# Sparse attention and a gated feed-forward on one core: a re-ordered lead-in, smaller weight pieces, a finer first output stage, and the last batch's transposes asked for earlier

## The chip, the cores and the metric

The kernel runs on one core of a Trainium2 chip. The metric is the time of one execution in microseconds on the device; of several runs the median is taken. One further execution was recorded by the hardware profiler. Times inside it count from the start of its span.

## The reference

Four batches of eight heads, 768 positions, head size 64. Every position attends to its neighbours within 15 positions and to one summary of each block of 32 positions: the summary key is the maximum over the block, the summary value the mean, and log 32 is added to its score. The joined heads go through a feed-forward with a gelu of the form h * sigmoid(1.702 h), without residual.

```python
k_sum = k.reshape(B, H, nb, block, D).max(axis=3)
v_sum = v.reshape(B, H, nb, block, D).mean(axis=3)
mask_l = np.abs(pos[:, None] - pos[None, :]) < window
scores_s = scale * np.einsum('bhsd,bhnd->bhsn', q, k_sum) + np.log(block)
a = softmax(concatenate([where(mask_l, scores_l, -1e9), scores_s]))
attn = np.matmul(a, concatenate([v, v_sum], axis=2))
x = attn.transpose(0, 2, 1, 3).reshape(B * S, H * D)     # 3072 x 512
h = x @ w_in                                             # 512 x 2048
out = (h / (1.0 + np.exp(-1.702 * h))) @ w_out           # 2048 x 512
```

q, k and v are 6.3 MB each in float32, the two weight matrices 4.2 MB each. Loads that are issued by GpSimd (POOL) change float32 to bfloat16 or float16 on the way.

## The kernel before, in words

The work is one long program, written out in the order in which each engine is to run it: every instruction of an engine stays in its program order. A batch is cut in two halves of 384 positions. "Pair" p is two heads (p = 0 to 3).

**Lead-in.** Batch 0, first half, is done pair by pair: keys and queries are turned on TensorE (`k_turn`, `q_turn`), copied from PSUM by ScalarE (ACT) or VectorE (DVE) (`k_own`, `q_copy`), the block maxima are taken on DVE (`k_max`), then scores (`s_bias`, `s_own`, `s_edges`), exponentials on ACT (`s_exp`), block scores (`b_turn`, `b_exp`), the sums of values over blocks as matmuls with a selector matrix E (`v_sum`, `v_copy`), products with values (`av_own`, `av_edges`, `av_blocks`), normalisation on DVE (`v_norm`), the turn of the result x (`x_turn`, `x_copy`), and the first two column groups of the first layer (`ff_first`). Matmuls on an array of zeros (`idle`) fill TensorE's waits at the start. The keys of pairs 0 and 1 come through SP's queue in float32 and are cast on ACT (`cast_k0`); all else comes through POOL's queue, in program order.

**First half of batch 0, feed-forward.** `ff_in(0, (nt,))` makes column group nt (128 of 2048) of the first layer: four matmuls of 384 columns and a gelu on ACT. The output stage `ff_out(0, ms, part)` takes row group ms (of three) and a quarter of the 2048 rows of w_out (four matmuls of 512 columns); it runs quarter by quarter, three row groups each, 12 slots. Beside these slots, `plan0` places the attention of batch 0's second half: late query turns ("q", `q_late`), scores ("s"), values and normalisation ("v"), the turn of x ("x", `tx`). Then `ff_in(1, ...)` runs the first layer of the second half, with the turns of batch 1's keys and queries between (`todo`), and `ff_out(1, ...)` its output, with batch 1's attention beside it (`plan1`).

**Batches 1 to 3.** Feed-forward of batch b with the attention of batch b + 1 beside the output products (`plan`); both layers' weights or sums of them enter a seven-product scheme (`w_sum`, `g_sums`, `product`). Keys, queries and x of batches 2 and 3 are turned by DMA transposes that SP issues: `xk` for keys, `xq` for queries, `dx` for x. SP issues strictly in order, and it issues the output stores and the DMAs that copy value rows (`value_rows`) too.

**Loads.** POOL issues, in this order: queries, keys and values of batch 0, w_in in five pieces, w_out in quarters with the four late query loads of batch 0 (`load_q1`) after the first quarter, the masks' arithmetic (`finish_masks`) ahead of the last quarter, then batch 1 (`load_batch(1)`). The program uses eight completion semaphores for these loads in turn, so that an issue waits for the landing of the load eight places ahead of it. Later batches are loaded by `load_batch(b)`, called from the output stage of the batch before; for batch 3 it waits (`gate2`) until batch 2's queries are turned.

Of the kernel before, what the change touches and what calls it, by code (L numbers as in the profile page):

```python
# [35 lines left out]
def kernel(  # L36
# [47 lines left out]
    RQ = 4  # L84
# [60 lines left out]
    E = consts.tile([128, EX + 128], BF16, name="E")  # L145
    ident16 = consts.tile([128, 128], F16, name="ident16")
    warm = lead.tile([128, 512], BF16, name="warm")
# [12 lines left out]
    def selectors():  # L160
        dve.memset(E, 0.0)
        for g in range(4):
            dve.memset(E[32 * g:32 * g + 32, EX + g:EX + g + 1], 1.0)

# [97 lines left out]
    def load_w_out(c):  # L262
        wo = moe_w_out.rearrange("(nt ni) d -> ni nt d", ni=128)
        pool.dma_start(out=w_out_sb[:, c * 4:(c + 1) * 4, :],
                       in_=wo[:, c * 4:(c + 1) * 4, :])
# [32 lines left out]
    def idle(n, cols=128):  # L298
# [82 lines left out]
    def k_turn(p):  # L381
        ps = st["K", p] = pturn.tile([128, 1024], BF16, name="ps_k", tag="turn")
        o = 2 * (p % 2)
        turn_plain(ps[:, 0:S], kb2[p // 2][:, o:o + 2])
# [16 lines left out]
    def q_turn(p):  # L401
        if p % 2 == 0:
            st["Q2"] = pturn.tile([128, 1024], BF16, name="ps_q", tag="turn")
        st["Q", p] = st["Q2"][:, p % 2 * HALF:p % 2 * HALF + HALF]
# [78 lines left out]
    def v_sum(ps_):  # L483

        for p in ps_:
            if p == 0:
                t = pturn.tile([128, 512], F32, name="ps_vt", tag="turn")
                st["VT", 0], st["VT", 1] = t[:, 0:2 * D], t[:, 2 * D:4 * D]
                st["VT", 0, 1] = t[:, 0:4 * D]
            elif p > 1:  # L490
                st["VT", p] = pturn.tile([128, 512], F32, name="ps_vt", tag="turn")[:, 0:2 * D]
            for i in range(2):
                for j in range(NJ):
                    o = EX - (p % 2 * 2 + i) * 32 - 4 * j
                    pe.matmul(out=st["VT", p][:, i * D:(i + 1) * D], lhsT=E[:, o:o + 128],
                              rhs=v0n[:, 2 * p + i, j, 0:D],
                              start=(j == 0), stop=(j == NJ - 1), skip_group_check=True)

    def v_copy(ps_, eng):
        h0, n = 2 * ps_[0], 2 * len(ps_)  # L500
        copy(eng, vs4[:, h0:h0 + n, 0:D], st[("VT",) + ps_].rearrange("p (h d) -> p h d", d=D))
# [367 lines left out]
    def ff_out(u, ms, part):  # L869
        if part == 0:  # L870
# [5 lines left out]
        if part == 3:  # L876
# [7 lines left out]
    gate3 = consts.tile([128, 2], F32, name="gate3")  # L884
    dve.memset(gate, 0.0)
# [9 lines left out]
    dve.memset(warm, 0.0)  # L895
# [25 lines left out]
    bands()  # L921
    dve.memset(v0n[:, :, :, D:VC], 1.0)
    clear_sums(dve)
    dve.tensor_copy(out=ident16, in_=ident)
# [10 lines left out]
    q_turn(1)  # L935
    s_bias(1)
    q_copy(0, dve)
    q_copy(1, dve)
    k_max(0)
    idle(8)  # L940
    s_own(0)
    s_own(1)
    s_edges(0)
    s_exp(0)
    s_edges(1)
    s_exp(1)
    k_max(1)
    k_turn(2)
    k_own(2, dve)
    b_turn(0)  # L950
    k_turn(3)
    k_own(3, act)
    b_exp(0)
    q_turn(2)
    q_turn(3)
    q_copy(2, dve)
    q_copy(3, dve)
    k_max(2)
    k_max(3)
    s_bias(2)  # L960
    s_bias(3)
    s_own(2)
    s_own(3)
    s_edges(2)
    s_exp(2)
    s_edges(3)
    s_exp(3)
    v_sum((0,))
    b_turn(1)
    b_exp(1)  # L970
    v_sum((1,))
    v_copy((0, 1), dve)
    av_own(0)
    av_own(1)
    av_edges(0)
    av_edges(1)
# [4 lines left out]
    v_sum((2,))  # L981
    v_copy((2,), act)
    av_own(2)
    av_edges(2)
    av_blocks(2)
    v_norm(2)
    v_sum((3,))
    v_copy((3,), act)
    av_own(3)
    av_edges(3)  # L990
    x_turn(0)
    x_copy(0, act)
    av_blocks(3)
    v_norm(3)
    x_turn(1)
    x_copy(1, act)
    x_turn(2)
    x_copy(2, act)
    ff_first(0)
    gelu_soon()  # L1000
    x_turn(3)
    ff_first(1)
    x_copy(3, dve)
    ff_first(2)
# [25 lines left out]
    plan0 = {1: ["q0", "q1", "q2"], 2: ["q3", "s0", "s1"], 4: ["s2", "s3"], 6: ["v0", "v1"], 8: ["x0"], 9: ["x1"]}  # L1030
# [221 lines left out]
```

## Time and profile before

| | |
|---|---|
| runs (us) | 206.19 (median), 205.59, 206.76 |
| profiled execution | 205.72 us, of which the span 203.7 |
| granted TensorE clock | 0.998 of full speed |
| lead-in, to the first whole first-layer group | about 0 to 20.7 us |
| batch 0: first half's first layer and output, second half's first layer and output | 20.7 to 29.8, to 44.5, to 57, to 74 |
| batch 1, batch 2, batch 3 (feed-forward) | from 74, 119, 163 |
| after the last matmul | about 3 us |

An engine's row in the profile gives its busy time, its share of the span and its number of instructions. PE is TensorE's matmuls, PEld its weight loads, SP the queue engine that does nothing but issue. A row of the chain of waits is start, duration, engine and what it writes, with the count of merged instructions. In the page's DMA row each digit is the busy share, in tenths, of the 16 DMA engines in one of 40 equal slices (5.1 us each). A row by windows gives the stretch, its length, busy time and count of PE, PEld, DVE, ACT and POOL, granted clock, DMA share and GB/s. Rows of a single load give the issuing engine, the load, the issue's duration (ns) and the first and last time of issue; the row under them gives the time from issue to landing (least, median, most). Rows "A <- B: total, times, longest" say that A stood idle until B was done.

### The profile page before, as it was taken

To read this page: it belongs to the slowest core of one execution; us is meant where nothing else is said; L and a number is where in the kernel's file an instruction comes from. 1 tells how busy PE (TensorE), PEld (TensorE's weight loads), DVE (VectorE), ACT (ScalarE), POOL (GpSimd) and SP (SyncE) were. 2 spreads that over 40 slices of the span, in tenths; PEclk is the share of its full clock that TensorE was granted. 3 is DMA by queue.
4 is the path that set the end of the run, shared out by engine and by line. 5 is a ranking of instruction groups with operands and counts; after the bars stand their busy time and mean duration, and the time that the engine had idled before them with its cause. 6 is when DMAs were issued, how large, how long until landed. Compare 5 with 4: busy or idle time off the path is not lost.

```text
span 203.7 us, 5850 instructions
## 1 busy us (share of the span) xinstructions
PE 196.8 (97%) x2358; PEld 136.7 (67%) x2358; DVE 141.6 (70%) x391; ACT 125.4 (62%) x240; POOL 90.3 (44%) x141
## 2 busy tenths in 40 slices
PE   6899999999999999999999999998999999999993
PEld 6567554556754665665888965666888855668882
DVE  6776885594855874897768689895769567758221
ACT  4674875539777617777871546778580568984220
POOL 7955489456899592002974035000000019870000
PEclk9999999999999999999999999999999999999999
DMA  6999999999999999999999979999022940000223
GB/s 179 159 164 204 207 210 218 184 156 240 107 157 149 185 181 165 139 162 156 118 185 146 154 125 137 130 241 180 0 106 52 172 140 3 0 0 0 106 105 103
DMA packets 95994, 28.13 MB, mean 138 GB/s; under 512 B 83664, under 2 KB 93152, under 8 KB 95968
## 3 DMA queue, kind: packets, MB, share of 16 engines
q0 software_dynamic: 69648, 13.24, 82.1%
q1 hardware_dynamic: 26176, 14.39, 34.9%
q8 instruction: 18, 0.29, 0.6%
q10 hardware_dynamic: 144, 0.13, 0.2%
q14 instruction: 8, 0.07, 0.1%
HBM read 27.26 MB, written 6.29 MB: 165 GB/s over the span
## 4 chain that ended last, share of the span: by engine, by line
PE 82%; DMA 9%; DVE 5%; ACT 1%; issue 1%; SPq 0%; ACTq 0%; DVEq 0%
PE ph L28 23%; PE poA L28 16%; PE po L28 11%; PE poB L28 8%; PE ps_av L28 4%; PE phA L28 4%; DMA out_dram<-osb 4%; PE poC L28 4%; PE ps_s L28 3%; DMA qT<-qb 3%; DMA gT<-in_k_dram 2%; DVE ks L28 2%; PE ps_t L28 1%; PE ps_x L28 1%; DVE qT L28 1%; DVE gs L28 1%
## 5 line engine op out<-in xcount | busy, mean ns | idle before, releaser
L28 PE MATMUL ph<-xT,w_in_sb 128*128 128x384 f16 x400 | 67.6, 326 | 0.1
L28 PEld LDWEIGHTS <-w_in_sb 128*128 128x128 f16 x442 | 42.7, 98 | 27.1 <-issue 0.2
L28 ACT ACTIVATE gT<-ph 128x384 f16<-128x384 f32 x100 | 47.9, 492 | 17.9 <-PE ph L28 17.1
L28 PEld LDWEIGHTS <-gT 128*128 128x128 f16 x312 | 28.8, 98 | 11.0
L28 ACT ACTIVATE a_sb<-ps_s 128x768 bf16<-128x768 f32 (+1 forms) x32 | 25.0, 826 | 12.1 <-PE ps_s L28 12.1
L28 PEld LDWEIGHTS <-gs 128*128 128x128 f16 x288 | 27.7, 98 | 3.4
L28 POOL DMA_DIRECT2D vw<-in_v_dram x36 | 24.6, 704 | 11.2 <-DMA kb<-in_k_dram 4.1
L28 POOL TENSOR_TENSOR gs<-gT 128x384 f16<-128x384 f16 x8 | 7.3, 911 | 43.1 <-PE phC L28 42.0
L28 PE MATMUL po<-w_out_sb,gT 128*128 128x512 f16 x96 | 23.6, 380 | 0.0
L28 DVE TENSOR_TENSOR a_sb<-a_sb,mk 128x768 bf16<-128x768 bf16 x28 | 14.9, 554 | 6.5 <-ACT a_sb L28 5.9
L28 PE MATMUL poA<-ws,gs 128*128 128x256 f16 x144 | 18.7, 273 | 0.0
L28 DVE TENSOR_TENSOR x<-ps_av,rc 128x384 f16<-128x384 f32 x32 | 17.8, 558 | 1.1
L28 DVE TENSOR_TENSOR gs<-gT 128x384 f16<-128x384 f16 (+1 forms) x34 | 13.3, 390 | 7.2 <-ACT gT L28 6.9
L28 POOL DMA_DIRECT2D qb<-in_q_dram x16 | 15.1, 964 | 3.1 <-DMA v0n<-in_v_dram 1.7
L28 PEld LDWEIGHTS <-kx 64*128 64x128 bf16 (+1 forms) x378 | 10.0, 95 | 7.8 <-issue 4.9
L28 DVE TENSOR_REDUCE ks<-kx 128x24 bf16<-128x768 bf16 x12 | 11.4, 948 | 3.4 <-ACT kx L28 3.2
L28 POOL DMA_DIRECT2D kb<-in_k_dram x14 | 13.6, 987 | 0.3 <-issue 0.3
L28 ACT ACT_TABLE_LOAD x10 | 12.8, 1283 | 1.0 <-PEq L1236 0.8
L28 ACT ACTIVATE osb<-poA 128x256 f32<-128x256 f32 x9 | 3.5, 384 | 15.8 <-PE poA L28 15.8
L28 ACT ACTIVATE s<-poA 128x256 f32<-128x256 f32 x11 | 4.2, 385 | 11.2 <-PE poA L28 11.2
L28 PEld LDWEIGHTS <-a_sb 128*64 128x64 bf16 (+2 forms) x400 | 7.8, 108 | 2.8 <-issue 1.3
L28 PE MATMUL poA<-w_out_sb,gT 128*128 128x256 f16 x72 | 9.4, 273 | 0.0
(117 smaller groups left out, 288.9 us busy)
## 6 DMA issues: line engine op xcount, KB each, us to landing
out_dram<-osb SPq DMA_DIRECT2D x22, 256.0 KB, 3.7
kb<-in_k_dram POOLq DMA_DIRECT2D x14, 192.0 KB, 6.6
qb<-in_q_dram POOLq DMA_DIRECT2D x12, 192.0 KB, 10.3
vw<-in_v_dram POOLq DMA_DIRECT2D x36, 64.0 KB, 5.5
w_out_sb<-in_moe_w_out_dram POOLq DMA_DIRECT2D x4, 512.0 KB, 13.0
w_in_sb<-in_moe_w_in_dram POOLq DMA_DIRECT2D x3, 512.0 KB, 12.8
vw<-vs SPq DMA_DIRECT2D x6, 198.0 KB, 6.7
gT<-in_k_dram SPq DMA_DIRECT2D x2, 384.0 KB, 3.5
```

The source lines that it names most:

```text
L28: r = f(*a, **kw)
```

## The change

- **Lead-in.** The keys of pairs 0 and 1 are cast into the layout in which two heads lie side by side, so that a turn takes 6 transposes of 128 x 128 (`turn_tiles`) instead of 12 of 128 x 64. The first half's queries lie as three rows on each of 128 partitions instead of four on 96. The array of zeros is float32, and the 40 idle matmuls (28, 4 and 8 of 128 columns) become 4 of 256 columns, 3 and 1 of 128. The block sums of values of pairs 0 and 1 are made by one run of six matmuls of 256 columns with a wider selector (`E4`), followed by a multiplication on DVE with a mask (`own`) that keeps each head's rows. `bands` on DVE moves behind the other constants; each pair's scores and exponentials follow each other; the first block scores (`b_turn(0)`) and the products with values take other places; x is turned earlier for pairs 0 and 1.
- **Weights.** w_in is loaded in eight pieces of 256 columns instead of two of 256 and three of 512; the first half of w_out in four pieces of two row groups, its second half in two quarters, with late queries between.
- **First output stage.** 24 slots of two matmuls instead of 12 of four. The second half's attention is spread over them anew. The last turn of x (x1) is taken out of it and put into `ff_in(1, range(3))`, between the first and the second half of the sums over the 512 input features.
- **Sums of w_out.** `w_sum` (DVE) moves to later places.
- **Batch 2's keys.** The first half of their load is issued beside `ff_in(1, (11,))` instead of in `load_batch(2)`.
- **Batch 3.** `xk` is called after products 8 and 10 instead of 16 and 18 of batch 1's output, `xq` after the third step of batch 2's first layer instead of the fifth.

POOL's loads around the weights, before:

```order
L28 DMA v0n<-in_v_dram 128x12x64 x4
L28 DMA w_in_sb<-in_moe_w_in_dram 128x4x256 x2
L28 DMA w_in_sb<-in_moe_w_in_dram 128x4x512 x3
L28 DMA w_out_sb<-in_moe_w_out_dram 128x4x512
L28 DMA qb<-in_q_dram 128x2x192 x4
L28 DMA w_out_sb<-in_moe_w_out_dram 128x4x512 x2
L28 MEMSET mk 128x128
```

Now (qb are the late queries; mk, the first row of the masks' arithmetic):

```order
L28 DMA v0n<-in_v_dram 128x12x64 x4
L28 DMA w_in_sb<-in_moe_w_in_dram 128x4x256 x8
L28 DMA w_out_sb<-in_moe_w_out_dram 128x2x512 x2
L28 DMA qb<-in_q_dram 128x2x192 x2
L28 DMA w_out_sb<-in_moe_w_out_dram 128x2x512
L28 MEMSET mk 128x128
```

and behind the masks' arithmetic, now:

```order
L28 AFFINE_SELECT mk<-mk 32x64
L28 DMA w_out_sb<-in_moe_w_out_dram 128x2x512
L28 DMA qb<-in_q_dram 128x2x192 x2
L28 DMA w_out_sb<-in_moe_w_out_dram 128x4x512 x2
L28 DMA kb<-in_k_dram 128x12x64 x4
L28 DMA qb<-in_q_dram 128x12x64 x2
```

where only the last quarter of w_out stood before. The pieces are smaller and half of the late queries stand later, but the second half of w_out still comes behind all of w_in, the first half of w_out and the four late query loads.

SP's queue in the output stage of batch 1, before (xT are the four x transposes for batch 2, kx the key transposes of batch 3, qT ahead of them the queries of batch 2):

```order
L28 DMA_TRANSPOSE qT_90<-qb 128x12x128 x2
L28 DMA out_dram<-osb 128x512 x2
L28 DMA_TRANSPOSE xT_98<-x_2258 128x6x128
L28 DMA out_dram<-osb 128x512
L28 DMA_TRANSPOSE xT_99<-x_2290 128x6x128
L28 DMA out_dram<-osb 128x512
L28 DMA_TRANSPOSE xT_100<-x_2355 128x6x128
L28 DMA_TRANSPOSE xT_101<-x_2387 128x6x128
L28 DMA_TRANSPOSE kx_89<-kb 128x12x64 x4
L28 DMA out_dram<-osb 128x512 x2
```

Now:

```order
L28 DMA_TRANSPOSE qT_92<-qb 128x12x128 x2
L28 DMA out_dram<-osb 128x512 x2
L28 DMA_TRANSPOSE kx_91<-kb 128x12x64 x4
L28 DMA_TRANSPOSE xT_100<-x_2211 128x6x128
L28 DMA out_dram<-osb 128x512
L28 DMA_TRANSPOSE xT_101<-x_2243 128x6x128
L28 DMA out_dram<-osb 128x512
L28 DMA_TRANSPOSE xT_102<-x_2308 128x6x128
L28 DMA_TRANSPOSE xT_103<-x_2340 128x6x128
L28 DMA out_dram<-osb 128x512 x2
```

The four key transposes moved from behind the last x transpose to ahead of the first.

The diff, cut to its core:

```diff
-    RQ = 4
+    RQ = 3
...
     def cast_k0(p):
         if p == 0:
-            kb2[0] = castp2.tile([128, 4, RK, D], BF16, name="kb", tag="kb")
-        act.activation(out=kb2[0][:, 2 * p:2 * p + 2].rearrange("p h r d -> p h (r d)"), in_=k0f[p], func=ACT.Copy)
+            kb2[0] = castp2.tile([128, 2, RK, 2, D], BF16, name="kb", tag="kb")
+        act.activation(out=kb2[0][:, p].rearrange("p r h d -> p h r d"),
+                       in_=k0f[p].rearrange("p h (r d) -> p h r d", d=D), func=ACT.Copy)
...
-    warm = lead.tile([128, 512], BF16, name="warm")
+    warm = lead.tile([128, 256], F32, name="warm")
...
+            dve.memset(E4[32 * g:32 * g + 32, 20 + g:20 + g + 97:32], 1.0)
+            dve.memset(own[32 * g:32 * g + 32, g], 1.0)
...
-        load_turned(k, b, kb2, "kb")
+        load_turned(k, b, kb2, "kb", (1,) if b == 2 else (0, 1))
...
+        if p < 2:
+            turn_tiles(ps, kb2[0][:, p], RK)
+        else:
+            turn_plain(ps[:, 0:S], kb2[1][:, 2 * p - 4:2 * p - 2])
...
+    def v_sum4():
+
+        ps = pturn.tile([128, 512], F32, name="ps_vt", tag="turn")[:, 0:4 * D].rearrange("p (h d) -> p h d", d=D)
+        for j in range(NJ):
+            pe.matmul(out=ps, lhsT=E4[:, 20 - 4 * j:148 - 4 * j], rhs=v0n[:, 0:4, j, 0:D],
+                      start=(j == 0), stop=(j == NJ - 1), skip_group_check=True)
+        dve.tensor_mul(vs4[:, 0:4, 0:D], ps, own.to_broadcast([128, 4, D]))
...
-    def ff_in(half, nts):
+    def ff_in(half, nts, between=None):
...
+            if between and part[0] == 0:
+                between()
...
-    def ff_out(u, ms, part):
+    def ff_out(u, ms, a, z):
...
-        for nt in range(4 * part, 4 * part + 4):
+        for nt in range(a, z):
...
-    for n0, n1 in ((0, 256), (256, 512), (512, 1024), (1024, 1536), (1536, 2048)):
-        load_w_in(n0, n1)
+    for n0 in range(0, d_ff, 256):
+        load_w_in(n0, n0 + 256)
     w50 = vw[0].rearrange("p (j e) h c -> p j e h c", e=2)
-    load_w_out(0)
-    for a in range(NP):
+    load_w_out(0, 2)
+    load_w_out(2, 4)
+    for a in range(2):
         load_q1(a)
-    for c in range(1, 3):
-        load_w_out(c)
+    load_w_out(4, 6)
     finish_masks()
-    load_w_out(3)
+    load_w_out(6, 8)
+    for a in range(2, NP):
+        load_q1(a)
+    for a in range(8, NT, 4):
+        load_w_out(a, a + 4)
...
-    idle(28)
+    idle(4, 256)
     k_turn(0)
-    k_own(0, act)
-    s_bias(0)
-    idle(4)
+    k_own(0, dve)
+    idle(3, 128)
     k_turn(1)
     k_own(1, act)
+    k_max(0)
+    idle(1, 128)
...
-    v_sum((0,))
+    av_own(0)
+    av_edges(0)
+    v_sum4()
+    dve.tensor_copy(out=ident16, in_=ident)
+    av_own(1)
+    av_edges(1)
     b_turn(1)
     b_exp(1)
...
-    plan0 = {1: ["q0", "q1", "q2"], 2: ["q3", "s0", "s1"], 4: ["s2", "s3"], 6: ["v0", "v1"], 8: ["x0"], 9: ["x1"]}
+    plan0 = {5: ["q0", "q1"], 8: ["s0", "s1"], 11: ["q2", "q3"], 14: ["s2", "s3"], 17: ["v0"], 20: ["v1", "x0"]}
...
-    for i, (ms, part) in enumerate((ms, part) for part in range(4) for ms in range(JH)):
-        ff_out(0, ms, part)
+    for i, (ms, a) in enumerate((ms, a) for a in range(0, NT, 2) for ms in range(JH)):
+        ff_out(0, ms, a, a + 2)
         beside0(i)
-        if i in (10, 11):
-            w_sum(i - 10, 0)
-            w_sum(i - 10, 1)
...
+            10: [lambda: w_sum(2, 1)], 9: [lambda: tq(0, 1, dve)], 11: [lambda: load_turned(k, 2, kb2, "kb", (0,)), lambda: tk(3, 1, act)], 12: [lambda: tq(1, 1, dve)],
...
-    ff_in(1, range(3))
+    ff_in(1, range(3), lambda: tx(1, 1))
...
+        if i in (10, 11):
+            w_sum(3, i - 10)
...
-                if n // 2 == 2 * b:
+                if n // 2 == 2:
                     xq(0, s)
                     xq(1, s)
...
-                if i in (16, 18):
-                    xk(i // 2 - 8, b % 2)
+                if i in (8, 10):
+                    xk(i // 2 - 4, b % 2)
```

More of the change, by code (lines that the diff above doesn't have):

```diff
@@ L260, in load_w_in, with load_w_out @@
         pool.dma_start(out=w_in_sb[:, :, n0:n1], in_=wi[:, :, n0:n1])
-    def load_w_out(c):
+    def load_w_out(a, z):
         wo = moe_w_out.rearrange("(nt ni) d -> ni nt d", ni=128)
-        pool.dma_start(out=w_out_sb[:, c * 4:(c + 1) * 4, :],
-                       in_=wo[:, c * 4:(c + 1) * 4, :])
+        pool.dma_start(out=w_out_sb[:, a:z, :], in_=wo[:, a:z, :])
     def copy(eng, out, in_):
@@ L296, in vsum, with idle @@
                               start=(j == 0), stop=(j == NJ - 1), skip_group_check=True)
-    def idle(n, cols=128):
+    def idle(n, cols):
         for i in range(n):
@@ L401, in q_turn @@
     def q_turn(p):
-        if p % 2 == 0:
-            st["Q2"] = pturn.tile([128, 1024], BF16, name="ps_q", tag="turn")
-        st["Q", p] = st["Q2"][:, p % 2 * HALF:p % 2 * HALF + HALF]
+        st["Q", p] = pturn.tile([128, 1024], BF16, name="ps_q", tag="turn")[:, 0:HALF]
         turn_plain(st["Q", p], qe[:, 2 * p:2 * p + 2])
@@ L481, in score_tiles, with v_sum @@
                           rhs=qT[p][s][r, i * QT:i * QT + QT], start=True, stop=True)
[L483 to L501, printed above, removed]
+    def v_sum4():
[4 more added lines that the diff above has]
+        dve.tensor_mul(vs4[:, 0:4, 0:D], ps, own.to_broadcast([128, 4, D]))
+    def v_sum(p):
+        ps = pturn.tile([128, 512], F32, name="ps_vt", tag="turn")[:, 0:2 * D]
+        for i in range(2):
+            for j in range(NJ):
+                o = EX - (p % 2 * 2 + i) * 32 - 4 * j
+                pe.matmul(out=ps[:, i * D:(i + 1) * D], lhsT=E[:, o:o + 128], rhs=v0n[:, 2 * p + i, j, 0:D],
+                          start=(j == 0), stop=(j == NJ - 1), skip_group_check=True)
+        copy(act, vs4[:, 2 * p:2 * p + 2, 0:D], ps.rearrange("p (h d) -> p h d", d=D))
     def pv_of(p):
@@ L884 @@
     gate3 = consts.tile([128, 2], F32, name="gate3")
+    dve.memset(warm, 0.0)
     dve.memset(gate, 0.0)
@@ L892, in exp_soon @@
         act.activation(out=gate[:, 1:2], in_=gate[:, 0:1], func=ACT.Exp)
-    dve.memset(warm, 0.0)
     dve.memset(wide, 0.0)
@@ L1112 @@
     for i, (ms, part) in enumerate((ms, part) for ms in range(JH) for part in range(4)):
-        ff_out(1, ms, part)
+        ff_out(1, ms, 4 * part, 4 * part + 4)
         beside(1, i)
+        if i in (10, 11):
+            w_sum(3, i - 10)
         if i == 2:
```

69 lines of the change are left out of this document (30 added, 39 removed).

## The prediction

> **What bounds the kernel now.** I read the page first, then the chain of work that ended last, then when the loads land.
>
> ```profile
> PE 196.8 (97%) x2358; PEld 136.7 (67%) x2358; DVE 141.6 (70%) x391; ACT 125.4 (62%) x240; POOL 90.3 (44%) x141
> DMA  6999999999999999999999979999022940000223
> PE 82%; DMA 9%; DVE 5%; ACT 1%; issue 1%; SPq 0%; ACTq 0%; DVEq 0%
> ```
>
> TensorE is busy for 196.8 of 203.7 us, so only about 7 us of idle time can be won without removing matmuls. But the second row says that the DMA engines are over 90% busy from the second slice (5 us) on, to the middle of the run: a second resource is nearly full beside TensorE. The chain of waits shows how TensorE spends the first 47 us:
>
> ```profile
> 8.28 1.73 DVE ks L28 x2
> 12.25 1.73 DVE ks L28 x2
> 19.76 10.08 PE ph L28 x62
> 31.56 0.62 PE ps_q L28 x18
> 36.28 0.46 PE ps_s L28 x24
> 36.73 1.83 PE po L28 x8
> 38.57 0.88 PE ps_av L28 x48
> 41.28 0.34 PE ps_x L28 x6
> 42.81 1.73 PE po L28 x8
> 44.54 2.60 PE ph L28 x16
> ```
>
> Two block maxima on DVE (1.73 each for two) hold the lead-in; from 19.76 on it is matmuls back to back. A first-layer matmul costs 10.08/62 = 0.163, an output matmul 1.73/8 = 0.216. What the weights do meanwhile stands in the answers on single loads (issue time in the first row of each pair, time to landing in the second; for w_in the last of the two):
>
> ```profile
> L28 POOL DMA_DIRECT2D w_in_sb<-in_moe_w_in_dram x2: 808/812/817, 10.9 to 11.7; - x2
> DMA to landing us min/median/max: 12.8/13.8/14.8
> L28 POOL DMA_DIRECT2D w_out_sb<-in_moe_w_out_dram x1: 742/742/742, 24.0 to 24.0; - x1
> DMA to landing us min/median/max: 13.3/13.3/13.3
> L28 POOL DMA_DIRECT2D w_out_sb<-in_moe_w_out_dram x1: 765/765/765, 30.3 to 30.3; - x1
> DMA to landing us min/median/max: 10.2/10.2/10.2
> ```
>
> So w_in is complete at 11.7 + 14.8 = 26.5, the third quarter of w_out lands at 24.0 + 13.3 = 37.3, the fourth at 30.3 + 10.2 = 40.5. The row at 36.73 is the sixth and seventh group of four output matmuls; the seventh, from 37.6 on, needs the third quarter: TensorE runs a few tenths behind the load stream, and no more. The first output stage is paced by two things at once, and an earlier start of TensorE meets the loads.
>
> **The change part by part.** The sum is made against the profiled execution: 205.72 us, of which 203.7 are the span. The three timed runs have a median of 206.19, that is 0.47 more; I add the terms to 205.72 and the 0.47 at the end.
>
> *Lead-in.* The warming matmuls become four wide float32 ones and four short ones instead of forty; two key groups are turned with 6 instead of 12 transposes each; the second pair of block maxima is waited for only behind the value products of the first two pairs. No row shows a float32 matmul; the nearest is the old row of 28, and the work that ends it:
>
> ```profile
> 1.31 3.17 PE L28 MATMUL ps_h<-warm 128*128 128x128 bf16 x28 [1.31 <-DVE warm L28]
> 3.81 0.84 ACT L28 ACTIVATE kb<-gT 128x768 bf16<-128x768 f32 x1 [1.49 <-DMA gT<-in_k_dram]
> ```
>
> The first keys are cast at 4.65. If the wide ones end by then they cost nothing; if they cost twice the old row (7.6) the lead-in is 3.0 late. I take nothing, by that nearest row: they stream fewer columns than 28 x 128, at a multiple of the cost that is unknown. On the other side, of the two waits for maxima one (1.73) goes at most; DVE still does all four, the copies of the keys and twelve more small memsets. Following each engine's new order with the durations of the rows I get the first whole first-layer group at 19.9 instead of 19.76 + 6 x 0.163 = 20.7: a gain of 0.8, bounds +3.0 late to 1.7 early. What follows decides whether it counts.
>
> *Weights in smaller pieces, output stage in 24 slots of two matmuls.* From 19.9, 56 matmuls end at 29.0; twelve slots (12 x 0.43 = 5.2), four query turns (24/18 x 0.62 = 0.8) and two score groups (0.46) end at 35.5. The next slot needs rows 8 to 11 of w_out. All that stood ahead of them in the load queue stands there still: the whole of w_in, half of w_out and all four late query loads. The engines are full, so they land where the third quarter landed, at 37.3. TensorE then waits 1.8 us, and this wait is the cover behind which the lead-in's gain, and any loss there up to 1.8, disappears.
>
> From 37.3: three slots 1.30, scores 0.46, three slots 1.30, v0 0.44 (half of 0.88): 40.8, just behind the last quarter at 40.5; three slots and v1: 42.5. Here the second change of the stage bites. The turn of the last x (x1) is moved from between the output matmuls, where it was covered, into the first three groups of the next stage, whose second half reads it. The DVE rows that price it:
>
> ```profile
> 39.11 0.20 DVE L28 RECIPROCAL rc<-ps_av 128x6 f32<-128x6 f32 x1 [0.40 <-PE ps_av L28]
> 41.42 0.56 DVE L28 TENSOR_TENSOR x<-ps_av,rc 128x384 f16<-128x384 f32 x1
> 41.90 0.55 DVE L28 COPY xT<-ps_x 128x768 f16<-128x768 f16 x1
> ```
>
> Normalising v0 and v1 took 39.11 to 41.98, 1.43 each. So v1 is normalised 1.53 after its matmuls, and DVE copies x0's turn only after that, done at 2.1; TensorE has x0's turn (0.34) and three slots (1.30), ends at 1.64 and waits 0.5. Six matmuls (0.98), x1's turn (0.34), then nothing to do while DVE copies (0.55 and two hand-overs of 0.04): 0.63. Six more (0.98) end at 42.5 + 5.1 = 47.6. Before, the same twelve matmuls ended at 44.54 + 12 x 0.163 = 46.5. **Term: +1.1.** Low end +0.5 (stream 0.4 sooner, by the 2.8 us between the landings of the two w_in rows, 23.7 and 26.5, against 3.2 between the two quarters of w_out, which are as large; and 0.2 less on DVE), high end +1.5 (stream 0.4 late).
>
> *Keys of batch 2, half of them asked for sooner.* Two loads are issued on POOL ahead of the last key's copies:
>
> ```profile
> 58.95 0.44 POOL L28 COPY kx<-ks 128x288 bf16<-128x288 bf16 x1
> 59.32 4.05 POOL L28 DMA_DIRECT2D kb<-in_k_dram  x4
> 62.49 0.35 PE L28 MATMUL ps_s<-qT,kx 64*128 64x64 bf16 x12
> ```
>
> Two issues are 2.0 us, so those copies end at 61.4 instead of 59.4; the scores that read them came at 62.5 and come later now. Nothing, and up to +0.3 if TensorE should be early. The weight sums that move on DVE have no reader for 30 us: nothing.
>
> *Batch 3 sooner on SP's queue.* Four key transposes go ahead of the four x transposes of the next first layer, and the query transposes are asked for two steps sooner.
>
> ```profile
> PE ps_s L28 <- DMA qT<-qb: 0.5, 1, 0.5
> 103.13 2.61 SPq L28 DMA_DIRECT2D out_dram<-osb  x2
> 110.23 1.23 SPq L28 DMA_TRANSPOSE xT<-x  x1
> 115.92 2.59 SPq L28 DMA_TRANSPOSE xT<-x  x2
> 118.84 3.91 PE ph L28 x24
> 119.08 6.78 SPq L28 DMA_TRANSPOSE kx<-kb  x4
> 120.22 0.72 POOL L28 CAST gate<-xT 128x1 bf16<-128x1 f16 x1 [10.98 <-DMA xT<-x]
> 134.24 5.91 SPq L28 DMA_TRANSPOSE qT<-qb  x2
> DMA to landing us min/median/max: 9.3/9.3/9.3
> ```
>
> The one wait of TensorE there, 0.5 for qT, goes: with 6.78 less ahead of it on SP the transpose starts some 4 us sooner. **Term: -0.5** (0 to -0.55). The price is queued behind the moved ones. SP is free of output stores at 105.7; four key transposes end at 112.5; the first x transpose leaves then instead of 110.2, and the last two end about 1.7 later than 118.5. The POOL row, which waits for the last x, shows it landed at 120.2; its reader comes 16 matmuls and two after 118.84, at 121.8. So 121.9 against 121.8: 0.1 if the key transposes run as quick as before. But value loads run beside them here, and the last row (the fourth key transpose, under query loads) shows one landing 9.3 after its issue. Bounds 0 to +2.5; **term +0.3**, near the low end, since the four were issued at an even 6.78/4 = 1.7 each.
>
> **Sum:** 1.1 - 0.5 + 0.3 = +0.9; 205.72 + 0.9 + 0.47 = 207.1.
>
> **Rivals.** *The gain arrives (faster).* If rows 8 to 11 of w_out land by 35.5, TensorE never waits for the stream: 35.5 + 5.2 (six slots, scores, v0, three slots, v1 as above) + 5.1 = 45.8 against 46.5, so -0.7, with -0.5 for qT -1.2: 205.0. For it: the quarter that might take 2.8 us took 3.2, so there is a slow stretch that smaller pieces might avoid. Against it: equal bytes through engines that the second row of the page shows full. Decided by that landing: the earlier than 36.5, the nearer to 205.
>
> *The x transposes come late (much slower).* If the key transposes' data take the 9.3 us of that last row, the first x lands near 121 where 118.84 needs it: +2.2 beside 1.1 - 0.5, 209.0.
>
> *The stream itself is slower.* The first queries go into 128 partitions in rows of 384 bytes instead of 96 partitions and 512 bytes. Rows of 384 bytes are in the trace already, the late queries, which moved in the second of these stretches:
>
> ```profile
> 28.00:30.00 2.00, 2.00 (x14) 1.17 (x12) 1.62 (x10) 1.62 (x5) 1.75 (x9) 1.00 1.48 210
> 30.00:32.00 2.00, 2.00 (x26) 1.00 (x23) 0.21 (x2) 1.85 (x3) 1.95 (x4) 1.00 1.28 204
> ```
>
> 204 against 210 GB/s (last column) is 3%, or 0.1 us over both query loads. If these rows were hit harder, say half as long again on some 2 us of loading, the whole stream is 1.0 late: 208.1. The Trainium skill, page "DMA: Bandwidth & Descriptors", section "Specifications", says that a transfer under 512 bytes does not reach line rate, since the engine then reads and writes back. By that rule this rival would be the forecast; the trace, at 204 against 210, disagrees so far.
>
> *It moves nothing.* DVE's hand-over overlaps better than I have it and the stream is a little sooner: the term is its low end +0.5, cancelled by qT: 206.2.
>
> **How the numbers follow.** Forecast 0.52, spread 206.0 to 208.2 by its bounds; gain arrives 0.18; x late 0.10; stream slower 0.07; nothing 0.13. A difference under 0.5% (1.03 us, 205.2 to 207.2) can't be told from none in a measurement of this kernel. The forecast lies close to that bound: I give 0.33 of it to slower, 0.19 to no change. Slower: 0.33 + 0.10 + 0.07 = 0.50; same: 0.19 + 0.13 = 0.32; faster 0.18. The range 204.9 to 208.6 leaves out about half of the first rival and most of the second.
>
> **What would show it.** In the changed profile: the first whole first-layer group near 19.9; a wait of TensorE of 1 to 2 us for a DMA of w_out near 36 to 37; the last w_out load landing near 40.5; two waits of 0.5 to 0.7 for DVE's copies of xT around 45 to 47; no wait for qT before batch 3's first scores; the last x transpose of batch 2 landing at most 1.5 later than before, relative to its first layer. I am wrong if w_out's third quarter lands before 36, if the x copies are covered, or if TensorE's waits in the first 48 us come to less than before.

## The result, and the profile after

The changed kernel takes 211.66 us (median of six runs, 209.69 to 212.08) against 206.24 (205.59 to 207.64) before: ratio 1.0244, interval 1.0206 to 1.0282, slower. The forecast of 207.1 had the direction and missed the size; its range ended at 208.6.

The profiled run is the quickest, 209.69 us with a span of 207.9 and a granted clock of 0.999. The other five have 210.28 to 212.08 at clocks of 0.998 to 0.982: this spread is part of the result. First the page of the changed kernel:

```profile
PE 198.3 (95%) x2296; PEld 136.7 (66%) x2296; DVE 141.4 (68%) x400; ACT 125.9 (61%) x241; POOL 94.3 (45%) x146
DMA  6999999999999999999999999991022860000222
PE 75%; DMA 11%; POOL 8%; DVE 2%; issue 2%; ACT 0%; POOLq 0%; ACTq 0%; DVEq 0%
```

The span is 4.2 us longer. TensorE's busy time is 1.5 more (198.3 against 196.8); 1.1 of this lies in the first 20 us, where idle matmuls stand in the place of waits, and what is lost behind them is idle time. GpSimd (POOL), which was not in the chain before, holds 8% of it. TensorE's waits say where:

```profile
PE po L28 <- DMA w_out_sb<-in_moe_w_out_dram: 2.1, 1, 2.1
PE ph L28 <- DVE xT L28: 1.4, 3, 0.6
PE ph L28 <- DMA xT<-x: 1.1, 1, 1.1
PE ph L28 <- ACT xT L28: 0.2, 1, 0.2
```

All four are new. The forecast had the first, two of the three in the second row and, at 0.3, the third. The chain of waits through the first output stage:

```profile
21.93 0.71 POOL qb L28
22.92 0.71 POOL w_out_sb L28
...
29.20 0.67 POOL w_out_sb L28
29.88 0.88 POOL qb L28 x2
30.75 0.54 issue
31.30 7.42 DMA w_out_sb<-in_moe_w_out_dram
38.76 1.46 PE po L28 x6
...
46.00 0.48 DVE xT L28
46.52 1.14 PE ph L28 x6
47.65 0.35 PE ps_x L28 x6
48.02 0.57 DVE xT L28
48.63 1.46 PE ph L28 x8
```

Read it from the middle: rows 8 to 11 of w_out land at 31.30 + 7.42 = 38.7, and what ended last ahead of that is not a load but GpSimd, which had asked for them at 31.3. The twelve matmuls of the second first-layer stage end six matmuls into the last row, at 49.6; before it was 46.5. So 3.1 of the 4.2 us are lost here, where the forecast had 1.1. GpSimd's timeline (start, duration, operation, count) shows what it did instead of asking; seven rows of mask arithmetic are left out:

```profile
22.92 0.71 POOL L28 DMA_DIRECT2D w_out_sb<-in_moe_w_out_dram  x1 [0.27 <-DMA w_in_sb<-in_moe_w_in_dram]
23.63 0.22 POOL L28 MEMSET mk<- 128x128 bf16 x1
...
28.97 0.23 POOL L28 TENSOR_SCALAR_AFFINE_SELECT mk<-mk 32x64 bf16<-32x64 bf16 x1
29.15 0.72 POOL L28 DMA_DIRECT2D w_out_sb<-in_moe_w_out_dram  x1
29.87 1.43 POOL L28 DMA_DIRECT2D qb<-in_q_dram  x2
31.30 1.51 POOL L28 DMA_DIRECT2D w_out_sb<-in_moe_w_out_dram  x2
```

Between 23.6 and 29.2 nothing is asked for. In the kernel before the third quarter was asked for at 24.0, ahead of the masks. The DMA engines' rate falls afterwards: 144 GB/s (last column) where the row of the same stretch before had 204:

```profile
30.00:32.00 2.00, 2.00 (x11) 0.89 (x10) 0.00 (x0) 1.87 (x3) 2.00 (x3) 1.00 0.91 144
```

### The profile page after: what moved, and what is told of

Same layout as the page of the kernel before. It is cut to its first block, busy times and chain, and to the rows that moved or that the text cites. A ratio compares the mean times of both kernels' runs of the same rounds, so it can differ in the third digit from the quotient of the medians.

```text
span 207.9 us, 5747 instructions
## 1 busy us (share of the span) xinstructions
PE 198.3 (95%) x2296; PEld 136.7 (66%) x2296; DVE 141.4 (68%) x400; ACT 125.9 (61%) x241; POOL 94.3 (45%) x146
## 4 chain that ended last, share of the span: by engine, by line
PE 75%; DMA 11%; POOL 8%; DVE 2%; issue 2%; ACT 0%; POOLq 0%; ACTq 0%; DVEq 0%
PE ph L28 25%; PE poA L28 15%; PE poB L28 8%; PE po L28 7%; DMA w_in_sb<-in_moe_w_in_dram 5%; PE phA L28 4%; PE poC L28 4%; DMA w_out_sb<-in_moe_w_out_dram 4%; PE ps_av L28 3%; PE ps_s L28 3%; POOL mk L28 2%; DMA xT<-x 2%; POOL v0n L28 2%; PE ps_t L28 1%; PE phB L28 1%
## 5 line engine op out<-in xcount | busy, mean ns | idle before, releaser
L28 PE MATMUL ph<-xT,w_in_sb 128*128 128x384 f16 x400 | 68.3, 326 | 2.7 <-DVE xT L28 1.4
L28 PE MATMUL po<-w_out_sb,gT 128*128 128x512 f16 x96 | 23.6, 380 | 2.1 <-DMA w_out_sb<-in_moe_w_out_dram 2.1
```

The source lines that it names most:

```text
L28: r = f(*a, **kw)
```

## The experiments

Medians of all runs in us, beside 206.1 to 206.2 for the kernel before on the same chips; "A" is the changed kernel, "B" the one before.

| run | kernel | median | lowest to highest |
|---|---|---|---|
| e1 | A + ten matmuls inside the wait | 209.70 | 209.56 to 211.05 |
| e2 | A + loads of B | 208.82 | 207.17 to 210.05 |
| e3 | A + turn of x1 back | 210.41 | 207.76 to 210.98 |
| e4 | A + keys of batch 3 back | 210.38 | 209.00 to 210.71 |
| e5 | A + masks behind the loads | 208.83 | 206.97 to 211.37 |
| e6 | A + edits of e2, e3 and e4 | 206.06 | 205.61 to 206.80 |
| e7 | B + queries of batch 3 sooner | 206.23 | 205.60 to 207.49 |
| e8 | B + lead-in of A | 205.44 | 204.55 to 206.33 |
| e9 | e1 + turn of x1 back | 209.80 | 209.39 to 211.23 |
| e10 | e1 + keys of batch 3 back | 208.89 | 208.55 to 210.88 |
| e11 | B + keys of batch 3 sooner | 209.09 | 207.04 to 210.01 |
| e12 | e8 + four first-layer groups begun early | 205.06 | 204.58 to 205.80 |
| e13 | e1 + turn and keys back | 208.55 | 208.07 to 208.86 |
| e14 | e5 + turn and keys back | 207.06 | 205.88 to 209.19 |
| e15 | e11 + stores on ScalarE's queue | 207.56 | 205.57 to 211.49 |

**The clock (e1).**

```diff
+        if i == 11:
+            spin = psb.tile([128, 1024], F32, name="spin", tag="big")
+            for n in range(10):
+                pe.matmul(out=spin[:, 0:512], lhsT=w_out_sb[:, 0, 0:128], rhs=w_out_sb[:, 1, :], start=True, stop=True)
```

> The changed kernel with ten 128x512 matmuls on data that is already there (2.2 us of TensorE), queued behind slot 11 of the first output stage, where TensorE stands still 2.1 us for rows 8 to 11 of w_out. Theory 'the clock': the wait itself costs 2.1 us in every run, and in most runs it also lowers the granted clock of TensorE afterwards, which makes the step from 209.7 (clock 0.999) to 212.1 (clock 0.98 to 0.99). Then the filled kernel has a clock of 0.998 or more in all runs and a median of 209.5 to 210.2. Rival 'the loads': the slower runs are slower because the loads land later in them; then the fill changes nothing, the median stays near 211.7 and the clock goes on varying between 0.98 and 1.00.

The median falls by 2.0 to 209.70, the time of the quickest run of the changed kernel, and the clock is 1.000 in all four runs (and 0.997 or more in the eight runs of e9 and e10 and the four of e13, which keep the extra matmuls). Nothing is removed, 2.2 us of work are added, and the kernel is faster; so most runs of the changed kernel, those with the low clocks, lose about 2 us here over the quickest one. How, the profile of e4 shows, which caught such a run. Its timeline, and its windows (the third number from the right is the granted clock):

```profile
39.57 2.72 PE L28 MATMUL po<-w_out_sb,gT 128*128 128x512 f16 x6 [3.15 <-DMA w_out_sb<-in_moe_w_out_dram]
```

```profile
39.00:40.00 1.00, 0.43 (x2) 0.16 (x2) 0.00 (x0) 0.00 (x0) 0.19 (x1) 0.76 1.24 204
40.00:41.00 1.00, 1.00 (x4) 0.40 (x3) 0.00 (x0) 0.00 (x0) 0.50 (x1) 0.50 1.79 173
41.00:42.00 1.00, 1.00 (x4) 0.15 (x1) 0.00 (x0) 0.00 (x0) 0.00 (x0) 0.50 2.33 159
42.00:43.00 1.00, 1.00 (x26) 0.69 (x26) 0.00 (x0) 0.24 (x1) 0.63 (x1) 0.53 2.44 156
43.00:44.00 1.00, 1.00 (x7) 0.47 (x6) 0.40 (x1) 1.00 (x2) 0.05 (x1) 1.00 2.45 156
```

Here w_out landed later than in the profiled run of the changed kernel, TensorE stood still for 3.15 instead of 2.15, and the six matmuls behind it took 2.72 instead of 1.46. The clock is 0.50 from 39.5 (0.76 is the mean of 0.52 at full and 0.48 at half) to 42.9: 3.4 us at half speed, in which 1.7 us of work are lost. The other 0.3 of e1's 2.0 are not traced; in e4 the wait itself is longer too, by 1.0.

**The loads (e2, e5).** In e2 the loads have the pieces and order of before (of the second part only the lines that come in are shown):

```diff
-    for n0 in range(0, d_ff, 256):
-        load_w_in(n0, n0 + 256)
+    for n0, n1 in ((0, 256), (256, 512), (512, 1024), (1024, 1536), (1536, 2048)):
+        load_w_in(n0, n1)
...
+    load_w_out(0, 4)
+    for a in range(NP):
+        load_q1(a)
+    load_w_out(4, 8)
+    load_w_out(8, 12)
+    finish_masks()
+    load_w_out(12, 16)
```

> The changed kernel with the loads of w_in, w_out and the late queries in the pieces and in the order of before (w_in in five, w_out in four quarters, the third quarter asked for ahead of the masks). Theory 'GpSimd asks too late': rows 8 to 11 land 1.4 later than forecast (38.7 instead of 37.3) because three of the loads ahead of them are asked for only behind 5.5 us of mask arithmetic; then the third quarter lands at 37.3 to 37.8 here, TensorE waits 0.7 to 1.2 instead of 2.1, the first twelve matmuls of the second first-layer stage end near 48.4 instead of 49.6, and the time is 208.3 to 208.7 in a run at full clock. Rival 'rows of 384 bytes of the first queries slow the stream': the landing stays within 0.3 of 38.7 and the time within 0.4 of 209.7.

In e5 the small pieces stay and one line moves:

```diff
-    finish_masks()
     load_w_out(6, 8)
     for a in range(2, NP):
         load_q1(a)
     for a in range(8, NT, 4):
         load_w_out(a, a + 4)
+    finish_masks()
```

> The changed kernel with its small weight pieces, but all of w_out and of the late queries asked for on GpSimd ahead of the masks instead of behind them. Theory 'GpSimd asks too late': rows 6 and 7 of w_out are asked for near 24 instead of 29.2 and rows 8 to 11 near 28.5 instead of 31.3; rows 8 to 11 land at 37.3 to 37.7 instead of 38.7, TensorE's wait for w_out falls from 2.1 to 0.8 to 1.3, and the time is 208.4 to 209.0 at a clock of 0.998 or more. Rival 'small pieces load slower': rows 8 to 11 land at 38.4 or later whatever the time of asking. Side effect for both: the masks end near 36 instead of 29, and if DVE's products with them hold v0 up, TensorE shows a new wait for a_sb near 40.

The time of asking is the cause. In e2 the third quarter lands at 24.37 + 13.3 = 37.7; TensorE now waits for the second quarter instead, 1.27 until 34.54, because the query turns and scores that stood ahead of it before stand behind it in the 24 slots. In e5 the small pieces, asked for in time, land 1.3 sooner, of which the stream was 0.3 ahead at its first piece of w_out (asked for at 17.17 against 17.52). Timeline of e5, GpSimd and then TensorE:

```profile
23.94 0.71 POOL L28 DMA_DIRECT2D w_out_sb<-in_moe_w_out_dram  x1 [0.61 <-DMA w_in_sb<-in_moe_w_in_dram]
...
28.40 0.76 POOL L28 DMA_DIRECT2D w_out_sb<-in_moe_w_out_dram  x1 [1.12 <-DMA w_out_sb<-in_moe_w_out_dram]
```

```profile
37.41 1.46 PE L28 MATMUL po<-w_out_sb,gT 128*128 128x512 f16 x6 [1.12 <-DMA w_out_sb<-in_moe_w_out_dram]
```

Rows 8 to 11 are asked for at 28.4, later than the third quarter before (24.0), and land as early as it did: GpSimd now asks for a load every 1.3 to 1.8 us all the way there, and from 30 to 32 us the engines move 197 GB/s instead of 144. The wait is halved, and the clock stays at 0.997 or more in all ten runs, without extra matmuls: one moved line gives 2.8 us, by the medians 2.0 that the extra matmuls give as well (e1) and 0.9 beyond. This profile is of the quickest of the ten runs; why others take up to 211.37 with the clock up is not shown. The wait for a_sb that the late masks might have brought does not come.

**The turn of x1 and the keys (e3, e4, e9, e10, e13).** Two edits: the first in e3 and e9, the second in e4 and e10, both in e13.

```diff
-    plan0 = {5: ["q0", "q1"], 8: ["s0", "s1"], 11: ["q2", "q3"], 14: ["s2", "s3"], 17: ["v0"], 20: ["v1", "x0"]}
+    plan0 = {5: ["q0", "q1"], 8: ["s0", "s1"], 11: ["q2", "q3"], 14: ["s2", "s3"], 17: ["v0"], 20: ["v1", "x0"], 23: ["x1"]}
-    ff_in(1, range(3), lambda: tx(1, 1))
+    ff_in(1, range(3))
```

```diff
-                if i in (8, 10):
-                    xk(i // 2 - 4, b % 2)
+                if i in (16, 18):
+                    xk(i // 2 - 8, b % 2)
```

> The changed kernel with the turn of the last x back between the output matmuls (behind slot 23), the first three groups of the next stage without it. Theory 'uncovered turn': TensorE's waits for DVE's copies of xT fall from 1.4 us (three) to 0.4 or less and the time by 0.8 to 1.0, to 208.7 to 208.9 at full clock. Rival 'the same wait further on': DVE is late with both copies anyway, the second half of the three groups waits for the second copy, and the time falls by 0.3 at most.

> The changed kernel with the key transposes of batch 3 back at their old places on SP (behind the x transposes), the query transposes left two steps sooner. Theory 'queue order': the wait of 1.1 us for the last x transpose of batch 2 goes, and the wait for the queries of batch 3 (0.5 in the kernel before) stays away; the time falls by 1.0 to 1.2, to 208.5 to 208.7 at full clock. Rival 'the x transposes are late because their inputs are': the wait stays above 0.7 and the time within 0.4 of 209.7. Second rival 'the queries need the keys out of the way': the xT wait goes and a wait of 0.5 or more for qT or kx ahead of batch 3's first scores comes.

> The changed kernel with the ten extra matmuls that keep the clock up (median 209.70 with these alone) and the turn of the last x back behind slot 23. With the clock out of the way this prices the uncovered turn alone. Theory: 0.9 less (the time from the landing of rows 8 to 11 to the end of the first twelve first-layer matmuls was 10.6 with and 9.8 without it): 208.7 to 208.9. Rival 'it only moves on': 209.4 or more, since the x transposes of batch 2 or the output buffers wait instead.

> The changed kernel with the ten extra matmuls that keep the clock up (median 209.70) and batch 3's key transposes back at their old places. This prices the order on SP's queue alone. Theory: the wait for the last x transpose of batch 2 (0.7 to 1.4 in the profiles so far) goes, 0.7 to 1.2 less: 208.5 to 209.0. Rival 'the forecast's term': 0.3 less, 209.4.

> The changed kernel with the ten extra matmuls that keep the clock up (209.70 with these alone), the turn of the last x behind slot 23 and batch 3's key transposes at their old places, both. One by one they gave 0 (209.80) and -0.8 (208.89). Theory 'they meet': with the keys early, TensorE's arrival at the end of batch 1's second layer is set by SP's queue, so that the turn's 1.0 only lengthens the wait there; with the keys back the turn counts in full: -0.8 - 1.0 = 207.9 or less. Rival 'the turn is covered anyway': 208.7 to 209.0, no more than the keys alone.

In e3 three of four runs, in e4 again three of four, have clocks of 0.989 to 0.992, so their medians mix two causes; e9, e10 and e13 hold the clock up. The keys alone give 0.8 there (e10, as expected). The turn alone gives nothing (e9), though its own waits go: from the landing of rows 8 to 11 to the end of the twelve matmuls it is 10.8 in the changed kernel (38.76 to 49.6) and 9.8 in e3 (38.06 to 47.8, twelve matmuls of 0.163 from 45.86). In e9's profile two things take back what it wins. Rows 8 to 11 land later, so that the stage goes on at 39.84, in e1 at 38.92. And at the end of batch 1's output TensorE waits 1.27 in two waits, where e1 has one of 0.66:

```profile
122.07 1.03 PE L28 MATMUL poA<-ws,gT 128*128 128x256 f16 x8 [0.88 <-DVE osb L28]
...
126.09 3.02 PE L28 MATMUL ph<-xT,w_in_sb 128*128 128x384 f16 x16 [0.39 <-DMA xT<-x]
```

DVE waits for an output buffer whose store, like the x transposes, stands on SP behind the four key transposes. With the keys back too (e13) the turn should count in full, 207.9 or less; it gives 0.3 more than the keys alone, which four runs each don't tell from none. Its waits are gone, but the ten extra matmuls hold the stage until 39.1, and its profile has a gap of 1.1 in TensorE at 71 that nothing in the trace explains. So that theory is supported by the waits and not by the size, and what the turn costs by itself stays open.

**All three (e6), and with small pieces (e14).**

> The changed kernel with three edits together: the loads in the pieces and the order of before, the turn of the last x back behind slot 23, batch 3's key transposes back at their old places. Left of the change are the lead-in, 24 slots, the half of batch 2's keys asked for sooner, the weight sums' places and the queries' transposes. Theory 'the causes add': 209.7 at full clock less 0.5 (loads; by the end of the first twelve matmuls in the run with the loads of before, 49.1 against 49.6), less 0.9 (turn), less 1.0 (keys): 207.3, every run at a clock of 0.998 or more. What is then still over the kernel before, 1 us, is the work beside the first output stage (query turns and scores) that stands behind the wait for the second quarter of w_out instead of ahead of it. Rival 'another wait takes over': the time is 208.2 or more, with a wait of TensorE of 0.7 or more that the changed kernel doesn't have.

> The changed kernel with its small weight pieces kept, but asked for ahead of the masks, and with the turn of the last x and batch 3's key transposes at their old places. With the loads of before instead of the small pieces these two gave 206.06. Theory 'the order of asking, not the size of the pieces': 205.8 to 206.4. Rival 'small pieces cost the stream': 206.8 or more, with rows 8 to 11 of w_out landing at 38 or later.

e6 takes 206.06, ratio 0.9985 (0.9949 to 1.0021): the whole 5.4 us are gone, 1.2 more than the single sums gave. These three edits undo the loss. That nothing else costs time does not follow: e6 keeps the lead-in, which alone wins 0.7 (e8, below), so that a cost of about 0.6 may hide behind it, and its profile has the wait that I expected to remain, for the second quarter of w_out:

```profile
PE po L28 <- DMA w_out_sb<-in_moe_w_out_dram: 0.7, 1, 0.7
```

e14 was to tell whether small pieces cost anything by themselves, and leaves it open: rows 8 to 11 land at 37.3, for the theory; the median is 207.06, for the rival; and its runs spread over 3.3 us, all at clocks of 0.997 or more.

**The parts put into the kernel before (e7, e8, e11, e15).** e7 asks for `xq` at `n // 2 == 2`, e8 takes over every edit above `first.close()` but the loads, e11 calls `xk` at 8 and 10.

> The kernel before with one edit: batch 3's query transposes asked for two steps sooner. Theory: TensorE's wait of 0.5 for qT goes, nothing else moves, 0.5 less than before (205.6 to 205.8 where before has 206.1 to 206.2). Rival: on SP they then stand ahead of the key and value transfers of the same stage, and these become late: 206.2 or more.

> The kernel before with the changed lead-in alone (whole-array key turns, wide idle matmuls, value sums, order of the lead-in, queries in rows of 384 bytes); loads, output stage and later queues as before. Theory 'the gain is lost inside the lead-in and the loads pace the rest': the first matmuls of the first layer start 0.7 to 1.0 sooner, the first whole group 0 to 0.2 sooner (TensorE waits 0.6 for the copies of x), the third and fourth quarter of w_out land within 0.4 of before, and the time is within 0.5 of before. Rival 'rows of 384 bytes slow the stream': w_out lands 0.4 to 1.0 later in all quarters and the time is 0.5 to 1.0 over before. Rival 'the lead-in's gain arrives': 0.5 to 0.8 under before.

> The kernel before with batch 3's key transposes alone asked for sooner (between the first output tiles of batch 1's second layer instead of near its end). Theory 'queue order': TensorE waits 0.7 to 1.2 for the x transposes of batch 2 or for an output buffer whose store stands behind the keys on SP, and the time is 0.6 to 1.2 over before. Rival 'the forecast's term': 0 to 0.4 over before.

e7: 206.23, ratio 1.0005 (0.9965 to 1.0045). The wait for qT is gone from the profile and the time has not moved; 0.5 is within the interval. e8: 205.44, ratio 0.9937 (0.9901 to 0.9973): the lead-in by itself makes the kernel faster by 0.6%, the last rival, against my theory. Its profile does not show where: it is of the slowest of the ten runs (206.33), and the first matmuls on x come at 18.6 there, hardly sooner than before. The rows of 384 bytes do not slow the stream in it: the quarters of w_out from the second on land at 33.5, 36.9 and 39.3, before at 34.1, 37.3 and 40.5. e11: 209.09, ratio 1.0123 (1.0031 to 1.0216): ten times the forecast's term. The waits and the chain of its profile, and SP's timeline:

```profile
PE poA L28 <- DVE osb L28: 2.3, 1, 2.3
```

```profile
115.97 4.53 DMA out_dram<-osb
...
120.62 0.43 DVE osb L28
121.05 0.04 issue
121.10 1.48 PE poA L28 x8
```

```profile
106.70 7.77 SPq L28 DMA_TRANSPOSE kx<-kb  x4
114.61 1.25 SPq L28 DMA_TRANSPOSE xT<-x  x1
115.97 0.52 SPq L28 DMA_DIRECT2D out_dram<-osb  x1
```

A store leaves at 115.97 instead of 112.25 (before) and lands at 120.5; DVE can't write the next output tile until then, and TensorE waits 2.3. The clock then falls here as well, from 121.5 to 124.9. In e15 the stores of batch 1 leave from ScalarE's queue:

```diff
-            queue.dma_start(out=out[r0:r0 + 128, cols], in_=now[t, o][:, cols])
+            (act if b == 1 else queue).dma_start(out=out[r0:r0 + 128, cols], in_=now[t, o][:, cols])
```

> The kernel before with batch 3's key transposes sooner, as in the run that cost 2.95, and with the output stores of batch 1 asked for on ScalarE's queue instead of on SP, so that they no longer stand behind the keys. Theory 'the stores are what is held up' (TensorE waited 2.3 for an output buffer, and its clock fell in two of four runs): that wait goes, the clock is 0.997 or more in all runs, and the time falls to 206.0 to 207.2, with up to 1 us of wait for the x transposes left. Rival 'the x transposes or the key data themselves': TensorE waits 1.5 or more for xT in place of the buffer and the time stays at 208 or more.

The result is split: five runs at 205.57 to 206.29, five at 208.83 to 211.49, the profiled one among these. The lower five by themselves are as fast as the kernel before, 0.9999 (0.9959 to 1.0039); of the upper five only two have a low clock (0.989 and 0.992). So the theory holds in half of the runs. The profile is of the other half. The wait that should have gone is there, and the rival's wait, for xT, is not:

```profile
PE poA L28 <- DVE osb L28: 2.2, 1, 2.2
```

A store asked for on the other queue at 112.68 still takes 8.7 to land, where the four stores ahead of the key transposes took 2.4 to 4.5 in the kernel before (first row: issue, second: landing):

```profile
112.68 0.34 ACTq L28 DMA_DIRECT2D out_dram<-osb  x1
DMA to landing us min/median/max: 8.7/8.7/8.7
```

The kernel before has such stores as well. This row is of its six stores from 103 to 127; the last two, asked for from 126.0 on, right behind the four key transposes, took 8.2 and 8.5:

```profile
DMA to landing us min/median/max: 2.4/4.3/8.5
```

So the place on SP's queue is not all of it. That key transposes in flight hold the stores' data up would fit both, but no run separates them from the other transfers; it stays open.

**A version that beats both (e12).** e8, with four instead of two first-layer groups begun x by x:

```diff
-    ff_first(0)
+    ff_first(0, (0, 1))
     x_turn(2)
     x_copy(2, act)
     gelu_soon()
-    ff_first(1)
-    ff_first(2)
+    ff_first(1, (0, 1))
+    ff_first(0, (2, 3))
     x_turn(3)
     x_copy(3, dve)
+    ff_first(1, (2, 3))
+    ff_first(2)
     ff_first(3)
```

> The kernel before with the changed lead-in and one addition: the first four (not two) first-layer groups are begun x by x in the lead-in, in a second accumulator pair, so that TensorE has four matmuls (0.65 us) to do while the third and the fourth x are copied. Theory: the waits of 0.2 and 0.45 for these copies go and the time is 0.3 to 0.6 under the lead-in alone (205.44), 204.9 to 205.1. Rival 'the loads pace the first output stage': TensorE only arrives sooner at the second quarter of w_out; the time is within 0.2 of the lead-in alone.

205.06, ratio 0.9937 (0.9907 to 0.9968) to the kernel before. TensorE's waits for the copies are gone (no idle time before these rows of e12; the rows of the changed kernel follow), but against e8 the difference, 0.4, can't be told from none: the two ratios are the same. Its profile has two waits for loads instead, the first two rows here, as the rival has it.

```profile
PE ph L28 <- DMA w_in_sb<-in_moe_w_in_dram: 0.4, 1, 0.4
PE po L28 <- DMA w_out_sb<-in_moe_w_out_dram: 0.3, 1, 0.3
18.64 1.05 PE L28 MATMUL ph<-xT,w_in_sb 128*128 128x384 f16 x4
19.53 0.33 PE L28 MATMUL ps_x<-ident,x 128*128 128x128 f16 x3
19.70 1.79 PE L28 MATMUL ph<-xT,w_in_sb 128*128 128x384 f16 x10
```

```profile
19.17 0.48 PE L28 MATMUL ph<-xT,w_in_sb 128*128 128x384 f16 x2 [0.18 <-ACT xT L28]
19.49 0.33 PE L28 MATMUL ps_x<-ident,x 128*128 128x128 f16 x3
20.27 3.90 PE L28 MATMUL ph<-xT,w_in_sb 128*128 128x384 f16 x23 [0.45 <-DVE xT L28]
```

## Why the prediction was too low, point by point

- **Lead-in, 0.8 sooner: did not arrive in the changed kernel, and was priced wrongly as worthless.** The first matmuls on x come 1.0 sooner (17.9 against 18.9), but the copies of x2 and x3 are then bare (0.18 and 0.45), and the first whole group starts at 20.6, as before. That the idle float32 matmuls cost next to nothing was right: the first keys are turned at 4.85 instead of 4.70. Alone (e8) the lead-in is worth 0.7 in the median, so that in the kernel before its gain does not disappear behind the loads; as e8's profile is of a slow run, whether TensorE or the loads come sooner in the others is not shown.
- **First output stage, +1.1: measured +3.1. This step failed first.** It said of the third quarter that "the engines are full, so they land where the third quarter landed, at 37.3". The same bytes stood ahead, but three of the loads ahead were asked for only behind the masks: 31.3 instead of 24.0 for rows 8 to 11. The page's busy digits, from which I took "full", say that something is in flight, not that enough is queued: the changed kernel's row has a 9 in the slices around 30 us too, and the rate of 144 GB/s says that not enough was. e5 undoes this with one line. Of the 2.0 by which the stage ended later than forecast (49.6 against 47.6) the landing is 1.4 (38.7 against 37.3). The rest is size: six output matmuls took 1.40 to 1.46 where the sum had 1.30, and the value products of v0 and v1 0.50 each where it had 0.44. The mechanism of the x1 term was right (waits of 0.31 and 0.65, forecast 0.5 and 0.63), though its price in the whole time is not shown alone (e9).
- **The clock, not in the sum: with the longer wait that brings it, about 2.0 of the 5.4.** I forecast a wait of 1.8 and asked only what it covers. It is 2.15 in the best run and over 3 in e4, and there TensorE runs at half speed for 3.4 us behind it, 1.7 us lost. e1, which fills the wait, wins 2.0.
- **Queries of batch 3, -0.5.** The wait went, as forecast. In the profiles the changed kernel is 4.4 behind in batch 2's first layer and 3.9 at the start of batch 3's (167.2 against 163.3), so the 0.5 arrives there; e7 alone, whose interval is wider than that, does not show it.
- **Keys of batch 3, +0.3 from bounds of 0 to +2.5: mis-sized.** In the profile of the changed kernel it is +1.1 (the wait for xT); by e10 0.8, and 2.95 alone in the kernel before, clock included. SP's issue times came out near the forecast (against the start of the first layer that reads it, the last x transpose is issued 1.1 later, forecast 1.7). What failed is the price by issue alone: the last x landed 3.2 behind the end of its issue (122.9 to 126.1), before 1.7. And the term left out the output stores on the same queue, whose three buffers DVE waits for.
- **Keys of batch 2 and w_sum, 0:** no wait for either in the profile.
- **The rivals.** "x transposes late" was the nearest in mechanism, and its 209.0 the nearest in time, but partly by luck: no rival had the late asking or the clock, which are the larger part of the loss. "The stream is slower" by 384-byte rows fell with e8. In e8 the bytes behind these rows landed no later. The rule cited from the Trainium skill, page "DMA: Bandwidth & Descriptors", section "Specifications", shows nothing here at this size.

## What to carry to other kernels

Ask of each load not only how many bytes stand ahead of it but when its engine gets round to asking: arithmetic on the issuing engine belongs behind the last load that someone waits for, and when loads are cut into smaller pieces, look at which of them now stand behind it. A wait of over 2 us on TensorE is not priced by its length alone, since the clock may fall behind it; a few matmuls on old data are a cheap guard and a cheap test. Before a transfer is moved ahead on a queue that issues in order, list everything that it passes, stores and their buffers included, and price their landings, not their issues.

## What the runs showed of the hardware that was not expected

TensorE's clock falls to 0.50 behind waits of 3.15 (e4), 2.34 (e11) and 2.23 us (e15, from 122.5 to 125.9) and stays there for 3.4 us in all three; behind one of 2.15 (the profiled run of the changed kernel) it stayed at 1.00. The Trainium skill, page "TensorE: Matmul & The Clock Gate", section "HAM oscillation — how this bites in real kernels", puts the limit at gaps of more than about 3.4 us. The three profiles differ: the clock fell behind shorter waits, 2.7 to 3.1 us after their start, when TensorE was at work again or just about to be. The time at half speed, 3.4 us, is what the same page states for the way back, in its section "Part 1: The HAM clock gate".
